# A two-layer linear-attention model on one core: query features of two tiles turned through DRAM and by DVE, and the second layer's output weights asked for at spaced places

## The chip, the core and the metric

The kernel runs on one NeuronCore of a Trainium2 chip. A core has TensorE (PE in the profile; PEld is its weight load, which runs beside the matmuls), VectorE (DVE), ScalarE (ACT), GpSimd (POOL) and SyncE (SP), which only issues transfers here. 16 DMA engines move data between DRAM and the on-chip memory; SP and ACT each have a queue of their own for issuing transfers, and a queue is worked off in order: an issue that waits for a semaphore holds up all issues behind it. The metric is device time in microseconds (us), as the median of several runs.

## What is computed

```python
x = A_x                                        # 1 x 2048 x 576, float32
for layer in range(2):                         # same weights in both layers
    q, k, v = split(layernorm(x) @ wqkv)       # 32 heads of 18
    phi_q = concat(softmax(q @ w_phi), softmax(-q @ w_phi))    # 36 features a head
    phi_k = the same of k
    kv, z = phi_k^T v, sum over rows of phi_k  # over all 2048 rows
    x = x + (phi_q kv) / (phi_q z + 1e-6) @ wo
    x = x + relu(layernorm(x) @ w1 + b1)^2 @ w2 + b2           # 576 -> 4608 -> 576
```

## The kernel before

**Tiles and blocks.** The 2048 rows are four blocks of 512, a block is four tiles of 128 rows. Matmuls run in a 32-bit format with two pieces, high and low, for each operand (names end in h and l), so that a product takes three matmuls.

**Dense parts.** `g_mlp` is the dense part (w1, square, w2) of one block: 36 turns, one for each 128 of the 4608 hidden features, f = 0 to 35. A turn has two steps. In `hidden(f)` PE makes 14 matmuls of 512 columns into one bank `ph` (L955), then ACT takes relu and square (L960, L961) and DVE splits the result (L964, L965). In `second(f-1)` PE multiplies the split result of the turn before by w2 (L980, L972). The weights of a turn come from DRAM on SP's queue: `m_1h` is the chunk of w1 (L918) and `m_1s` that of w2 (L930) in the dense part of block 1, each in two buffers, so a chunk can be loaded when the step that used the chunk two turns before has ended. Only the very first dense part ("fresh", block 3 of layer 0) loads the plain weights (`m_3rr`), splits them on ACT and DVE (L914, L915, L926, L927) and writes the pieces to DRAM for later.

**What is woven in.** While PE works on the dense part of one block, the attention of the next block is woven in. `weave` runs one slot of a `Plan` after each step of the dense part, and a plan's turn is two slots. `plan_attend` puts the calls at turns: query features of the four tiles (`exponents`, `totals`, `scaled`, nearly all DVE), then for each of 5 head groups and 2 signs (i = 0 to 9) the features turned so that features lie on partitions, then `times` (L776) with the blocks of the keys, then `project` (L799) with the output weights wo, then the norm for the block's own dense part. A call with a larger depth stands earlier within its slot. In each engine the order is that of the program, except on SP, whose order a scheduler makes from when it takes each transfer to be ready. There are three such dense parts in each layer (the fourth has no next block). In layer 0 the second and third also hold the keys of the second layer for the block just finished (`plan_keys`).

**The two ways to turn.** In layer 0 `Out.turn` (L714 to L716) transposes the four tiles on PE into a bank, ACT copies the high piece out and DVE makes the low one. In layer 1 a tile makes a trip: `arrange` (POOL) copies the features into a padded tile z, `store` sends z to the DRAM tensor `phs` from ACT's queue (L737), `fetch` brings it back with 32x32 blocks in their place (L742), `flip` lets DVE transpose each 32x32 block (L747), and `pieces` takes high and low pieces of each tile (L756, L757). The fetched tile (`e`) uses the buffers `wraw` and `rr`, in which the output weights come later: `a_0o0h` is the high piece of the first half of wo's columns for block 0, then `a_0o0l`, `a_0o1h`, `a_0o1l` (L315, two transfers each).

Of the kernel before, what the change touches and what calls it, by code (L numbers as in the profile page):

```python
# [7 lines left out]
F32 = mybir.dt.float32  # L8
F32R = mybir.dt.float32r
AF = mybir.ActivationFunctionType  # L10
# [3 lines left out]
P = 128  # L14
TB = 512
NT = TB // P
# [5 lines left out]
def layers_kernel(  # L22
# [18 lines left out]
    nc = tc.nc  # L41
# [653 lines left out]
    class Out:  # L695

        def __init__(self, layer, b, ph, name):
            self.layer, self.b, self.ph, self.name = layer, b, ph, name
            self.f, self.pn, self.x, self.pair = {}, {}, {}, None
            self.z, self.e = {}, {}  # L700

        def turn(self, i, half=None):
            g, s = divmod(i, 2)
# [34 lines left out]
                                    self.z.pop((t, s)).rearrange("p (a f) -> p a f", a=KC))  # L738

        def fetch(self, t):  # L740
            self.e[t] = sb.tile([P, NC * HP], F32, tag=TAGS_C[t % 2], name=f"{self.name}e{t}")
            nc.scalar.dma_start(self.e[t][:, : KC * 2 * NG * 32],  # L742
                                phs[self.b][t].rearrange("a (r k) s f -> (a r) (k s f)", k=KC))

        def flip(self, t):
            e = self.e[t][:, : KC * 2 * NG * 32]
            nc.vector.transpose(e, e)  # L747

        def pieces(self, i):
            g, s = divmod(i, 2)  # L750
            w = gw[g]
            fh, fl = (sb.tile([GW, TB], F32R, tag="ft", name=f"{self.name}f{k}{g}{s}", bufs=4) for k in "hl")
            for t in range(NT):
                src = self.e[t][:w, : KC * 2 * NG * 32].rearrange("p (k n r) -> p k n r", k=KC, r=32)[:, :, s * NG + g]
                hi, lo = (f[:w, t * P : (t + 1) * P].rearrange("p (r k) -> p k r", k=KC) for f in (fh, fl))
                nc.scalar.activation(hi, src, AF.Copy)  # L756
                nc.vector.tensor_sub(lo, src, hi.bitcast(F32))  # L757
            self.f[i] = fh, fl

        def times(self, i, half=None):  # L760
# [56 lines left out]
    def plan_queries(plan, at, gap, layer, raws, er, ph, name):  # L817

        zb = sums[layer]["zb"]
        r = {}  # L820

        def first(t):
            if t == 0:
                r[0] = sb.tile([P, NT, 2, H], F32, tag="rq", name=f"{name}r", bufs=1)
            er.append(exponents(raws[t], f"{name}Q{t}"))

        def second(t):
            e, rt = er[t], r[0][:, t]
            totals(e, rt)
            m = sb.tile([P, 2, D], F32, tag="m", name=f"{name}m{t}", bufs=1)  # L830
            u = sb.tile([P, 2, H], F32, tag="u", name=f"{name}u{t}", bufs=1)
            nc.vector.tensor_mul(m, e, zb)
            nc.vector.tensor_reduce(u, m.rearrange("p s (h d) -> p s h d", d=DH), op=ALU.add, axis=AX.X)
            r[t + 1] = u

        def third(t):
            e, rt, u = er[t], r[0][:, t], r.pop(t + 1)
            nc.vector.tensor_mul(u, u, rt)
            nc.vector.scalar_tensor_tensor(u[:, 0], u[:, 0], DEN_EPS, u[:, 1], op0=ALU.add, op1=ALU.add)
            nc.vector.reciprocal(u[:, 1], u[:, 0])  # L840
            nc.vector.tensor_mul(rt, rt, u[:, 1].unsqueeze(1).to_broadcast([P, 2, H]))
            scaled(e, rt)
            ph.append(e)

        for t in range(NT):
            plan.put(at + gap * t, 0, first, t)
            plan.put(at + gap * t + 1, 1, second, t)
            plan.put(at + gap * t + 2, 2, third, t)
        return at + gap * (NT - 1) + 2

    def plan_attend(plan, at, gap, layer, b, raws, dst, name, o, queries=None):

        out = Out(layer, b, [], name)
        out.pair, calls = o
        if queries:
            for t in range(NT):
                plan.put(at + gap * t, 0, queries, t)
            at += 1
        if layer == 0:
            for n, call in enumerate(calls):  # L860
                plan.put(at + n, 9, call)
        done = at + 2
        at = plan_queries(plan, at, gap, layer, raws, [], out.ph, name) + 1
        if layer:
            for t in range(NT):
                for k, (step, call) in enumerate(((0.5, out.arrange), (1.5, out.store), (2.5, out.fetch), (4, out.flip))):
                    plan.put(done + gap * t + step, -1, call, t)
            at += 3.5
        for i in range(2 * NG):
            plan.put(at + i / 2, 0, out.pieces if layer else out.turn, i)  # L870
            plan.put(at + (i + 1 + layer) / 2, 1, out.times, i)
        if layer:
            for n, call in enumerate(calls):
                plan.put(at + NG + n / 4, 9, call)
            at += 1.5
        at += NG + 1
        for t in range(NT):
            plan.put(at + t - 1, 9, out.load, t)
        trips = range(NT) if layer else range(NT - 1)
# [547 lines left out]
    def body():  # L1427

        order = [NB - 1, NB - 2] + list(range(NB - 2))
        queries, other, o, last_keys = opening()  # L1430
        for layer in range(2):
            q1 = None
            ready, prev_rows, keep = {}, None, {}
            for i, b in enumerate(order):
                n = f"{layer}_{b}"
                nxt, rows = {}, []
                gen = g_mlp(layer, b, ready, rows, f"m{n}", layer == 0 and i == 0, i == 0, layer == 1 and i == NB - 1)
                plan = Plan()
                if i == 0:
                    out = Out(layer, b, [], f"t{layer}o")  # L1440
                    out.pair = o[0]
                    barrier(layer, b, last_keys, queries, other, ready, out, gen)
                    for t in range(NT):
                        plan.on(2 + t, 0, out.keep, t, out.x[t])
                at = 0
                if prev_rows is not None:
                    at = plan_keys(plan, prev_rows, i == NB - 1, keep)
                if i + 1 < NB:
                    nb, n2 = order[i + 1], f"a{layer}_{order[i + 1]}"
                    if i or layer:  # L1450
# [90 lines left out]
```

## Time and profile before

| what | value |
|---|---|
| median of 3 runs | 2523.01 us (2520.92 to 2524.05) |
| profiled execution | 2526.71 us |
| its span, first to last instruction | 2525.0 us |
| mean granted clock of TensorE | 0.996 |
| PE busy | 2495.7 us (99%) |
| DVE, ACT, POOL busy | 1223.7, 769.7, 152.5 us |
| bytes moved | 540.99 MB, mean 214 GB/s |

The profiled execution is 3.7 us above the median and 1.7 us longer than its span. PE is nearly always busy, so the places where it is not, and the instructions that it issues, are what to read; the other engines matter where PE waits for them. The first dense part runs from about 240 to 490 us, the three of layer 1 with a woven attention from about 1465 to 2290 us.

### The profile page before, as it was taken

Reading aid. Unit: us, or ns where it says so; the run is one execution under the profiler, and the core shown is the slowest. Engines: PE = TensorE matmul, PEld = TensorE weight load, DVE = VectorE, ACT = ScalarE, POOL = GpSimd, SP = SyncE. Lnnn points to the kernel's source line nnn. Section 1 sums busy time; section 2 is a strip of 40 time slices with the busy share of each in tenths; the row PEclk is TensorE's granted clock in tenths of the full one; section 3 lists DMA queues with packets and bytes.
Section 4 is the critical chain, followed back from the end, with each engine's and each line's share of the span. In section 5 each row is a group of like instructions: output and inputs, shape, how many; then the busy total and the mean of one; then the engine's idle time right before and its main releaser. Section 6 shows DMA issues by size and latency. Waiting matters only on the chain.

```text
span 2525.0 us, 37453 instructions
## 1 busy us (share of the span) xinstructions
PE 2495.7 (99%) x15084; PEld 2198.6 (87%) x15084; DVE 1223.7 (48%) x2115; ACT 769.7 (30%) x1358; POOL 152.5 (6%) x419
## 2 busy tenths in 40 slices
PE   9999999999999999999999999999999999999999
PEld 8998888898888988888889988788887888888887
DVE  6887955444635446355114776433463426433112
ACT  5544443322222222223223332313223222312221
POOL 4302000000000000000000011000010002000000
PEclk9999999999999999999999999999999999999999
DMA  9514888867648576484564348668575767667665
GB/s 318 175 53 135 288 279 283 307 230 268 215 157 288 179 255 207 165 292 146 193 196 158 130 139 268 215 196 281 177 254 181 259 225 239 206 204 247 197 195 171
DMA packets 196619, 540.99 MB, mean 214 GB/s; under 512 B 26270, under 2 KB 79390, under 8 KB 196446
## 3 DMA queue, kind: packets, MB, share of 16 engines
q1 hardware_dynamic: 163806, 511.06, 60.8%
q10 hardware_dynamic: 32640, 27.53, 3.4%
q8 instruction: 120, 1.97, 0.3%
q14 instruction: 53, 0.43, 0.0%
HBM read 440.12 MB, written 98.40 MB: 213 GB/s over the span
## 4 chain that ended last, share of the span: by engine, by line
PE 97%; DMA 2%; DVE 1%; ACT 0%; issue 0%; SPq 0%; DVEq 0%; ACTq 0%
PE m_2ph L955 9%; PE m_0ph L955 9%; PE m_1ph L955 9%; PE m_3ph L955 9%; PE m_2acc L980 7%; PE m_1acc L980 7%; PE m_3acc L980 7%; PE m_0acc L980 7%; PE m_2acc L972 2%; PE m_1acc L972 2%; PE m_0acc L972 2%; PE m_3acc L972 2%; PE a_0po L799 1%; PE a_2po L799 1%; PE kvp L598 1%; PE a_3po L799 1%
## 5 line engine op out<-in xcount | busy, mean ns | idle before, releaser
L955 PE MATMUL m_0ph<-a_0nh,m_0h 128*128 128x512 f32 x720 | 226.8, 397 | 5.6 <-DMA m_0h<-dw 5.6
L955 PE MATMUL m_2ph<-a_2nh,m_2h 128*128 128x512 f32 x720 | 225.4, 395 | 0.0
L980 PE MATMUL m_1acc<-m_1s,m_1hb 128*128 128x448 f32 x864 | 189.0, 367 | 0.4 <-PE m_1ph L955 0.4
L980 PE MATMUL m_2acc<-m_2s,m_2hb 128*128 128x448 f32 x864 | 189.3, 367 | 0.0
L980 PE MATMUL m_3acc<-m_3s,m_3hb 128*128 128x448 f32 x864 | 188.9, 367 | 0.3 <-DVE m_3hb L964 0.3
L980 PE MATMUL m_0acc<-m_0s,m_0hb 128*128 128x448 f32 x864 | 189.0, 367 | 0.0
L964 DVE CAST m_2hb<-m_2hr 128x512 fp32r<-128x512 f32 x72 | 30.8, 427 | 311.1 <-ACT m_2hr L961 310.7
L980 PEld LDWEIGHTS m_1acc<-m_1s,m_1hb 128*128 128x128 f32 x864 | 161.9, 188 | 18.7 <-PE m_1ph L955 0.5
L980 PEld LDWEIGHTS m_3acc<-m_3s,m_3hb 128*128 128x128 f32 x864 | 161.2, 188 | 17.4 <-PE m_3ph L955 0.5
L980 PEld LDWEIGHTS m_2acc<-m_2s,m_2hb 128*128 128x128 f32 x864 | 160.9, 188 | 16.1
L980 PEld LDWEIGHTS m_0acc<-m_0s,m_0hb 128*128 128x128 f32 x864 | 160.5, 188 | 15.4
L955 PEld LDWEIGHTS m_0ph<-a_0nh,m_0h 128*128 128x128 f32 x720 | 136.1, 189 | 37.4 <-issue 6.2
L964 DVE CAST m_0hb<-m_0hr 128x512 fp32r<-128x512 f32 x72 | 30.8, 428 | 273.4 <-ACT m_0hr L961 273.0
L955 PEld LDWEIGHTS m_2ph<-a_2nh,m_2h 128*128 128x128 f32 x720 | 135.3, 188 | 30.4
L960 ACT ACTIVATE m_0hr<-m_0ph,b1t 128x512 f32<-128x512 f32 x72 | 49.6, 689 | 353.9 <-PE m_0ph L955 343.8
L964 DVE CAST m_1hb<-m_1hr 128x512 fp32r<-128x512 f32 x72 | 30.7, 427 | 260.7 <-ACT m_1hr L961 260.7
L960 ACT ACTIVATE m_2hr<-m_2ph,b1t 128x512 f32<-128x512 f32 x72 | 49.6, 689 | 346.5 <-PE m_2ph L955 346.5
L960 ACT ACTIVATE m_1hr<-m_1ph,b1t 128x512 f32<-128x512 f32 x72 | 49.6, 689 | 324.5 <-PE m_1ph L955 314.4
L960 ACT ACTIVATE m_3hr<-m_3ph,b1t 128x512 f32<-128x512 f32 x72 | 49.6, 689 | 263.4 <-PE m_3ph L955 263.4
L964 DVE CAST m_3hb<-m_3hr 128x512 fp32r<-128x512 f32 x72 | 30.7, 426 | 197.7 <-ACT m_3hr L961 197.7
L955 PE MATMUL m_1ph<-t1onh,m_1h 128*128 128x512 f32 (+1 forms) x380 | 114.2, 387 | 5.6 <-DMA m_1h<-dw 4.9
L955 PE MATMUL m_3ph<-a_3nh,m_3h 128*128 128x512 f32 x360 | 114.7, 401 | 4.4 <-DMA m_3h<-dw 4.4
(1992 smaller groups left out, 5686.6 us busy)
## 6 DMA issues: line engine op xcount, KB each, us to landing
m_2h<-dw SPq DMA_DIRECT2D x72, 640.0 KB
m_0h<-dw SPq DMA_DIRECT2D x72, 640.0 KB
m_1h<-dw SPq DMA_DIRECT2D x72, 640.0 KB
m_2s<-dw SPq DMA_DIRECT2D x72, 576.0 KB
m_0s<-dw SPq DMA_DIRECT2D x72, 576.0 KB
m_1s<-dw SPq DMA_DIRECT2D x72, 576.0 KB
dw<-m_3h SPq DMA_DIRECT2D x36, 640.0 KB
m_3h<-dw SPq DMA_DIRECT2D x36, 640.0 KB
```

What stands on the lines that cost most here:

```text
L598: nc.tensor.matmul(po[32 * q : 32 * q + 32, :, j], vt[:, h * VW : h * VW + 32], e[:, :, h * DH : (h + 1) * DH], start=not stay, stop=True, ...
L799: nc.tensor.matmul(pt[:, :HP], a, m[:w, g], start=(g == 0 and k == 0), stop=(g == NG - 1 and k == 2))
L955: nc.tensor.matmul(ph[:, cols], a, m, start=(k == 0), stop=(k == 3 * KC + 1))
L960: nc.scalar.activation(hr, ph, AF.Relu, bias=b1t[:, f : f + 1])
L964: nc.vector.tensor_copy(hh, hr)
L972: nc.tensor.matmul(acc[KC], a, m, start=(f == 0 and k == 0), stop=(f == NF - 1 and k == 2))
L980: nc.tensor.matmul(acc[t][:, :R], a[:, rows], m, start=(f == 0 and k == 0), stop=(f == NF - 1 and k == 2))
```

## The change

In layer 0 tiles 0 and 1 of each of the three woven attentions now make the trip; tiles 2 and 3 are still transposed on PE, side by side in one bank (`pieces` does both). Their fetched tiles use buffers `v`, one for each sign (640 columns instead of 1280). `times` of layer 0 comes a slot later after its pieces, and all that follows it half a turn later. In layer 1 all four tiles go through DRAM as before; their flip is planned 1 turn after the fetch instead of 1.5, and the four requests for output weights, which stood at +0, +0.25, +0.5 and +0.75 turn, now stand at -0.5, +0.5, +1 and +2; `project` and the norm follow one turn later. In the last two woven dense parts of layer 1 the queries start at turn 5 instead of 6.5, and the four transfers of the normalised rows that they need are put 1 turn apart instead of 1.5.

```diff
         def fetch(self, t):
+            n = NG * 32
+            if len(self.trips) == NT:
+                e = self.e[t, 0] = self.e[t, 1] = sb.tile([P, NC * HP], F32, tag=TAGS_C[t % 2], ...)
...
+            for s in range(2):
+                e = self.e[t, s] = sb.tile([P, KC * n], F32, tag="v", name=f"{self.name}e{t}{s}", bufs=4)
+                nc.scalar.dma_start(e.rearrange("p (k f) -> p k f", k=KC),
+                                    phs[self.b][t][:, :, s].rearrange("a (r k) f -> (a r) k f", k=KC))
...
         def pieces(self, i):
-            for t in range(NT):
+            for t in self.trips:
...
                 nc.scalar.activation(hi, src, AF.Copy)
                 nc.vector.tensor_sub(lo, src, hi.bitcast(F32))
+            if n < NT:
+                pt = wtile(f"{self.name}pt{g}{s}")
+                for t in range(n, NT):
+                    nc.tensor.transpose(pt[:w, t * P : (t + 1) * P], self.ph[t][:, s, g * GW : g * GW + w], ident)
+                nc.scalar.activation(fh[:w, n * P :], pt[:w, n * P :], AF.Copy)
+                nc.vector.tensor_sub(fl[:w, n * P :], pt[:w, n * P :], fh[:w, n * P :].bitcast(F32))
...
+        out.trips = range(NT if layer else 2)
+        back = 2.5 if layer else gap + 0.5
+        for t in out.trips:
+            plan.put(done + gap * t + 0.5, -1, out.arrange, t)
+            plan.put(done + gap * t + 1.5, -1, out.store, t)
+            plan.put(done + gap * t + back, -2, out.fetch, t)
+            plan.put(done + gap * t + back + 1, -1, out.flip, t)
         if layer:
-            at += 3.5
+            at += 3
         for i in range(2 * NG):
-            plan.put(at + i / 2, 0, out.pieces if layer else out.turn, i)
-            plan.put(at + (i + 1 + layer) / 2, 1, out.times, i)
+            plan.put(at + i / 2, 0, out.pieces, i)
+            plan.put(at + i / 2 + 1, 1, out.times, i)
+        at += 0.5
         if layer:
             for n, call in enumerate(calls):
-                plan.put(at + NG + n / 4, 9, call)
-            at += 1.5
+                plan.put(at + NG + (-0.5, 0.5, 1, 2)[n], 9, call)
+            at += 2.5
...
-                        start, step = (at - 4, 0.5) if at else (0, 0.75)
+                        start, step = (at - 4 if at else 0), 0.5
...
-                        plan_attend(plan, at or 6.5, 2, layer, nb, raws2, nxt, n2, o,
+                        plan_attend(plan, at or 5, 2, layer, nb, raws2, nxt, n2, o,
```

**SP, first woven dense part of layer 1.** Issues in SP's queue before (h and s are the weight chunks, the number behind them the turn; o0h to o1l the output weights):

```order
L918 DMA m_1h_23_15739<-dw_23_156 128x1280
L930 DMA m_1s_22_15722<-dw_22_191 128x1152
L315 DMA a_0o0h<-kept_oh 126x1152
L315 DMA a_0o0h<-kept_oh 72x288
L315 DMA a_0o0l<-kept_ol 126x1152
L315 DMA a_0o0l<-kept_ol 72x288
L315 DMA a_0o1h<-kept_oh 126x1152
L930 DMA m_1s_23_15785<-dw_23_192 128x1152
L315 DMA a_0o1h<-kept_oh 72x288
L315 DMA a_0o1l<-kept_ol 126x1152
L315 DMA a_0o1l<-kept_ol 72x288
L918 DMA m_1h_24_15800<-dw_24_157 128x1280
```

And now, in the same place of SP's queue:

```order
L945 DMA m_1h_23_15939<-dw_23_156 128x1280
L315 DMA a_0o0h<-kept_oh 126x1152
L957 DMA m_1s_22_15929<-dw_22_191 128x1152
L315 DMA a_0o0h<-kept_oh 72x288
L315 DMA a_0o0l<-kept_ol 126x1152
L315 DMA a_0o0l<-kept_ol 72x288
L945 DMA m_1h_24_15986<-dw_24_157 128x1280
L957 DMA m_1s_23_15982<-dw_23_192 128x1152
L315 DMA a_0o1h<-kept_oh 126x1152
L315 DMA a_0o1h<-kept_oh 72x288
L945 DMA m_1h_25_16030<-dw_25_158 128x1280
L957 DMA m_1s_24_16028<-dw_24_193 128x1152
```

Chunk h 24 stood behind all four output pieces and s 23; now it stands behind o0h and o0l only and ahead of s 23, o1h stands behind s 23, and o1l comes after s 24. In the two later dense parts of layer 1 the order is the same, with 26 in the place of 24.

**PE, first woven attention of layer 0**, the end of a `second`, the transposes of i = 0 and the start of `hidden(14)`, before:

```order
L972 MATMUL m_3acc_3708<-m_3hb_4330,m_3s_12_4292 128x512 x3
L714 MATMUL a_2pt_4408<-ident,a_2Q0e 126x128
L714 MATMUL a_2pt_4408<-ident,a_2Q1e 126x128
L714 MATMUL a_2pt_4408<-ident,a_2Q2e 126x128
L714 MATMUL a_2pt_4408<-ident,a_2Q3e 126x128
L955 MATMUL m_3ph_4424<-t0onh,m_3h_14_4362 128x512
```

And now:

```order
L999 MATMUL m_3acc_3708<-m_3hb_4374,m_3s_12_4336 128x512 x3
L777 MATMUL a_2pt_4456<-ident,a_2Q2e 126x128
L777 MATMUL a_2pt_4456<-ident,a_2Q3e 126x128
L982 MATMUL m_3ph_4470<-t0onh,m_3h_14_4406 128x512
L982 MATMUL m_3ph_4470<-t0onl,m_3h_14_4406 128x512
```

Two of four transposes are gone in each of 30 groups: PE has 8224 rows instead of 8284.

**DVE, the same attention**, before (L915 makes the low piece of the chunk of w1 for turn 9, L964 and L965 split the square of `hidden(8)`, L927 makes the low piece of the chunk of w2, L561 starts on the features of tile 2):

```order
L915 TENSOR_TENSOR m_3h_9_4087<-m_3rr_4027,m_3h_9_4087 128x640
L964 CAST m_3hb_4109<-m_3hr_4106 128x512
L965 TENSOR_TENSOR m_3hb_4109<-m_3hr_4106,m_3hb_4109 128x512
L927 TENSOR_TENSOR m_3s_9_4127<-m_3rr_4027,m_3s_9_4127 128x576
L561 TENSOR_REDUCE a_2r<-a_2Q2e 128x64
```

And now, with the first flip (the two rows of L757):

```order
L942 TENSOR_TENSOR m_3h_9_4121<-m_3rr_4043,m_3h_9_4121 128x640
L991 CAST m_3hb_4143<-m_3hr_4140 128x512
L992 TENSOR_TENSOR m_3hb_4143<-m_3hr_4140,m_3hb_4143 128x512
L757 STREAM_TRANSPOSE a_2e_4087<-a_2e_4087 128x640
L757 STREAM_TRANSPOSE a_2e_4089<-a_2e_4089 128x640
L954 TENSOR_TENSOR m_3s_9_4165<-m_3rr_4043,m_3s_9_4165 128x576
L561 TENSOR_REDUCE a_2r<-a_2Q2e 128x64
L562 RECIPROCAL a_2r<-a_2r 128x64
```

The fetch that this flip needs is issued on ACT's queue one turn earlier, right behind the square of `hidden(7)`. The flip of tile 1 stands at the same place three turns later.

More of the change, by code (lines that the diff above doesn't have):

```diff
@@ L699, in __init__ @@
             self.f, self.pn, self.x, self.pair = {}, {}, {}, None
-            self.z, self.e = {}, {}
+            self.z, self.e, self.trips = {}, {}, ()
         def turn(self, i, half=None):
@@ L740, in fetch, with turned @@
         def fetch(self, t):
-            self.e[t] = sb.tile([P, NC * HP], F32, tag=TAGS_C[t % 2], name=f"{self.name}e{t}")
-            nc.scalar.dma_start(self.e[t][:, : KC * 2 * NG * 32],
-                                phs[self.b][t].rearrange("a (r k) s f -> (a r) (k s f)", k=KC))
-        def flip(self, t):
-            e = self.e[t][:, : KC * 2 * NG * 32]
-            nc.vector.transpose(e, e)
+            n = NG * 32
+            if len(self.trips) == NT:
+                e = self.e[t, 0] = self.e[t, 1] = sb.tile([P, NC * HP], F32, tag=TAGS_C[t % 2], name=f"{self.name}e{t}")
+                nc.scalar.dma_start(e[:, : KC * 2 * n], phs[self.b][t].rearrange("a (r k) s f -> (a r) (k s f)", k=KC))
+                return
+            for s in range(2):
+                e = self.e[t, s] = sb.tile([P, KC * n], F32, tag="v", name=f"{self.name}e{t}{s}", bufs=4)
+                nc.scalar.dma_start(e.rearrange("p (k f) -> p k f", k=KC),
+                                    phs[self.b][t][:, :, s].rearrange("a (r k) f -> (a r) k f", k=KC))
+        def flip(self, t):
+            if len(self.trips) == NT:
+                e = self.e[t, 0][:, : KC * 2 * NG * 32]
+                nc.vector.transpose(e, e)
+                return
+            for s in range(2):
+                nc.vector.transpose(self.e[t, s], self.e[t, s])
+        def turned(self, t, s, g, w):
+            e = self.e[t, s]
+            if len(self.trips) == NT:
+                return e[:w, : KC * 2 * NG * 32].rearrange("p (k n r) -> p k n r", k=KC, r=32)[:, :, s * NG + g]
+            return e[:w].rearrange("p (k n r) -> p k n r", k=KC, r=32)[:, :, g]
         def pieces(self, i):
             g, s = divmod(i, 2)
-            w = gw[g]
+            w, n = gw[g], len(self.trips)
             fh, fl = (sb.tile([GW, TB], F32R, tag="ft", name=f"{self.name}f{k}{g}{s}", bufs=4) for k in "hl")
-            for t in range(NT):
-                src = self.e[t][:w, : KC * 2 * NG * 32].rearrange("p (k n r) -> p k n r", k=KC, r=32)[:, :, s * NG + g]
+            for t in self.trips:
+                src = self.turned(t, s, g, w)
                 hi, lo = (f[:w, t * P : (t + 1) * P].rearrange("p (r k) -> p k r", k=KC) for f in (fh, fl))
@@ L863, in plan_attend @@
         at = plan_queries(plan, at, gap, layer, raws, [], out.ph, name) + 1
+        out.trips = range(NT if layer else 2)
[5 more added lines that the diff above has]
+            plan.put(done + gap * t + back + 1, -1, out.flip, t)
         if layer:
-            for t in range(NT):
-                for k, (step, call) in enumerate(((0.5, out.arrange), (1.5, out.store), (2.5, out.fetch), (4, out.flip))):
-                    plan.put(done + gap * t + step, -1, call, t)
-            at += 3.5
+            at += 3
         for i in range(2 * NG):
-            plan.put(at + i / 2, 0, out.pieces if layer else out.turn, i)
-            plan.put(at + (i + 1 + layer) / 2, 1, out.times, i)
+            plan.put(at + i / 2, 0, out.pieces, i)
+            plan.put(at + i / 2 + 1, 1, out.times, i)
+        at += 0.5
         if layer:
             for n, call in enumerate(calls):
-                plan.put(at + NG + n / 4, 9, call)
-            at += 1.5
+                plan.put(at + NG + (-0.5, 0.5, 1, 2)[n], 9, call)
+            at += 2.5
         at += NG + 1
```

## The prediction

> **What bounds the kernel.** I read the page's busy times first, then the chain of waits, then who PE waits for.
>
> ```profile
> PE 2495.7 (99%) x15084; PEld 2198.6 (87%) x15084; DVE 1223.7 (48%) x2115; ACT 769.7 (30%) x1358; POOL 152.5 (6%) x419
> PE 97%; DMA 2%; DVE 1%; ACT 0%; issue 0%; SPq 0%; DVEq 0%; ACTq 0%
> ```
>
> PE is busy or on the chain nearly all the time. So two things can shorten the span: instructions that PE no longer issues, and the few waits of PE. What falls on DVE, ACT, POOL or the queues counts only if PE comes to wait for it. PE's longest waits, all of them in layer 1:
>
> ```profile
> PE m_0ph L955 <- DMA m_0h<-dw: 5.6, 1, 5.6
> PE m_1ph L955 <- DMA m_1h<-dw: 4.9, 1, 4.9
> PE m_3ph L955 <- DMA m_3h<-dw: 4.4, 1, 4.4
> PE fp L219 <- DMA fr<-in_A_wqkv: 1.5, 2, 0.8
> ```
>
> Each woven dense part of layer 1 has one wait for a chunk of w1, 4.4 to 5.6 us, and the next largest wait in the kernel is 1.5 us in two pieces. The timeline of PE shows that the wait is not all (first a `hidden` step without a wait and the step behind it, then for each of the three waits the step that waited and the one behind it):
>
> ```profile
> 1629.58 0.40 PE L955 MATMUL m_1ph<-t1onh,m_1h 128*128 128x512 f32 x1
> ...
> 1632.85 2.60 PE L980 MATMUL m_1acc<-m_1s,m_1hb 128*128 128x448 f32 x12
> ...
> 1641.06 0.77 PE L955 MATMUL m_1ph<-t1onh,m_1h 128*128 128x512 f32 x1 [4.92 <-DMA m_1h<-dw]
> ...
> 1646.67 2.60 PE L980 MATMUL m_1acc<-m_1s,m_1hb 128*128 128x448 f32 x12
> ...
> 1942.77 0.76 PE L955 MATMUL m_0ph<-a_0nh,m_0h 128*128 128x512 f32 x1 [5.63 <-DMA m_0h<-dw]
> ...
> 1947.76 0.29 PE L799 MATMUL a_3po<-a_3o0h,a_3oh 126*128 126x288 f32 x1
> ...
> 2217.13 0.76 PE L955 MATMUL m_3ph<-a_3nh,m_3h 128*128 128x512 f32 x1 [4.37 <-DMA m_3h<-dw]
> ...
> 2223.09 0.29 PE L799 MATMUL a_2po<-a_2o0h,a_2oh 126*128 126x288 f32 x1
> ```
>
> A `hidden` of 14 matmuls takes 1632.85 - 1629.58 = 3.27 us. Behind the waits it takes 5.61, 4.99 and 5.96 us. The reason is in the windows (columns: stretch, its length, busy time of PE, PEld, DVE, ACT and POOL, then granted clock, share of the DMA engines, GB/s):
>
> ```profile
> 1638.00:1642.00 4.00, 0.94 (x2) 0.83 (x3) 0.00 (x0) 0.00 (x0) 0.00 (x0) 0.65 0.96 364
> 1642.00:1646.00 4.00, 4.00 (x11) 3.08 (x10) 0.00 (x0) 0.00 (x0) 0.00 (x0) 0.50 0.14 54
> ```
>
> After the wait the granted clock is 0.50 for the whole of 1642 to 1646, so PE pays a second time. The Trainium skill, "TensorE: Matmul & The Clock Gate", Part 1, says that the clock falls to half once PE has been idle for a window of about 3.4 us; the three waits, all longer, agree with it.
>
> Why the chunk is late stands in SP's queue (issues; the chunk that waits is the last row):
>
> ```profile
> 1623.66 0.76 SPq L315 DMA_DIRECT2D a_0o0h<-kept_oh  x2
> ...
> 1629.07 0.34 SPq L930 DMA_DIRECT2D m_1s<-dw  x1
> ...
> 1630.74 0.35 SPq L918 DMA_DIRECT2D m_1h<-dw  x1
> ```
>
> The output weights go out as soon as the fetched tiles are free; then the queue stands still until 1629.07, when PE ends the `second` that frees a buffer for m_1s; m_1h, whose own buffer was free when the `hidden` before had ended (about 1625), is issued only at 1630.74 and lands when PE starts, at 1641. So it is late twice: 5.4 us in the queue, then 10 us behind a full set of transfers.
>
> **The change, part by part.**
>
> *Output weights spaced.* h 24 (26 in the two later parts) now stands behind o0h and o0l only, ahead of the s that blocked it. How long it takes is worked out from sizes:
>
> ```profile
> m_1h<-dw SPq DMA_DIRECT2D x3, 640.0 KB
> m_1s<-dw SPq DMA_DIRECT2D x4, 576.0 KB
> a_0o0h<-kept_oh SPq DMA_DIRECT2D x1, 567.0 KB
> a_0o0h<-kept_oh SPq DMA_DIRECT2D x1, 81.0 KB
> ```
>
> From the issue of o0h on there lie two pieces of 648 KB, one s of 576 KB and h itself with 640: 2512 KB or 2.57 MB, at the 364 GB/s of the window above 7.1 us. Between o0h's issue and the `hidden` that needs this h lie more than two steps of dense part with their `times`: before, 1623.66 to 1636 (wait begins), 12.3 us, and now the same or more, since the pieces end just after a `hidden` and h is needed by the third `hidden` after it. So it arrives about 5 us early. The next two chunks each have one s and one output piece (1224 KB, 3.4 us) ahead of them and a turn to come in: 3.27 us of `hidden` and as much of `second` (1632.85 to 1641.06 - 4.92 = 1636.14), 6.6 us. o1l goes out two turns before `project` needs it, about 13 us. I take all three waits as gone: 4.92 + 5.63 + 4.37 = 14.92 us, and the slow matmuls with them: (5.61 - 3.27) + (4.99 - 3.27) + (5.96 - 3.27) = 6.75 us. Together 21.7 us; the bounds are 0 (another chunk is late by as much) and 21.7.
>
> *Transposes on PE.* Three attentions of layer 0 times 10 groups lose two of four transposes: 60. Their price is the spacing of starts, not the duration:
>
> ```profile
> 326.11 0.27 PE L714 MATMUL a_2pt<-ident,a_2Q0e 128*126 128x128 f32 x1
> ...
> 326.44 0.27 PE L714 MATMUL a_2pt<-ident,a_2Q3e 128*126 128x128 f32 x1
> ```
>
> 0.33 us for three steps, 0.11 us each, so 60 x 0.11 = 6.6 us off PE. That time is on the path, because PE is.
>
> *Pieces in layer 0 on ACT and DVE.* Before and now, for one group:
>
> ```profile
> L715 ACT ACTIVATE a_0fh<-a_0pt x10: 579/594/599, 685.2 to 723.2; 126x512 fp32r<-126x512 f32 x8, 72x512 fp32r<-72x512 f32 x2
> L756 ACT ACTIVATE a_0fh<-a_0e x40: 416/440/449, 1589.0 to 1623.2; 126x128 fp32r<-126x128 f32 x32, 72x128 fp32r<-72x128 f32 x8
> L715 ACT ACTIVATE t0of<-t0opt x20: 370/382/391, 200.7 to 221.3; 126x256 fp32r<-126x256 f32 x16, 72x256 fp32r<-72x256 f32 x4
> 335.00:345.00 10.00, 10.00 (x53) 8.67 (x52) 5.08 (x9) 5.33 (x9) 0.00 (x0) 1.00 0.92 299
> ```
>
> ACT: 0.59 us becomes 2 x 0.44 + 0.38 = 1.26, so +6.7 us an attention; DVE's subtractions follow ACT's pieces and grow alike. This falls in some 40 us in which ACT is busy 5.33 of 10 us and DVE 5.08 (the last row). `times` now has two slots instead of one behind its pieces. I cost it at nothing; if the cover went, PE would wait in `times`, at most 6.7 us an attention.
>
> *Stores, fetches, flips in layer 0.* POOL's arranging (POOL stands idle in these rows) costs nothing. The place to watch is the first dense part, where DVE is nearly full:
>
> ```profile
> 285.00:295.00 10.00, 10.00 (x47) 8.57 (x47) 8.47 (x13) 5.01 (x7) 0.00 (x0) 1.00 0.84 270
> 295.00:305.00 10.00, 10.00 (x47) 8.46 (x46) 9.29 (x16) 3.95 (x6) 0.00 (x0) 1.00 0.76 278
> L747 DVE STREAM_TRANSPOSE a_0e<-a_0e x4: 1503/1504/1511, 1529.0 to 1586.1; 128x1280 f32<-128x1280 f32 x4
> 290.71 0.76 DVE L927 TENSOR_TENSOR m_3s<-m_3rr,m_3s 128x576 fp32r<-128x576 f32 x1 [1.13 <-ACT m_3s L926]
> 291.77 1.35 DVE L561 TENSOR_REDUCE a_2r<-a_2Q2e 128x64 f32<-128x1152 f32 x1 [0.30 <-ACT a_2Q2e L558]
> ...
> 297.41 0.69 DVE L965 TENSOR_TENSOR m_3hb<-m_3hr,m_3hb 128x512 fp32r<-128x512 f32 x1
> 281.20 0.63 ACT L961 ACTIVATE m_3hr<-m_3hr 128x512 f32<-128x512 f32 x1
> 299.62 0.69 ACT L960 ACTIVATE m_3hr<-m_3ph,b1t 128x512 f32<-128x512 f32 x1 [1.89 <-PE m_3ph L955]
> ```
>
> A flip of 1280 columns takes 1.50 us; two of 640 I put at 1.6. The first one stands just in front of L927 at 290.71, where DVE idles 1.13 us and, a step on, 0.30. Behind it waits the split that ends at 297.41 + 0.69 = 298.1, which PE needs when `hidden(10)` is over, at 299.6 (ACT's relu of it starts then). So DVE may run 1.5 us late there before PE waits. If the fetched tile is there, DVE runs 1.6 - 1.43 = 0.2 us late and PE loses nothing. Whether it is there: the fetch goes out behind ACT's square, at 281.8, and DVE reaches the flip at 290.71 - 1.13 = 289.6, 7.8 us later. The one fetch of which the trace shows the landing:
>
> ```profile
> 1577.80 0.34 ACTq L742 DMA_DIRECT2D a_0e<-phs  x1
> 1586.07 1.51 DVE L747 STREAM_TRANSPOSE a_0e<-a_0e 128x1280 f32<-128x1280 f32 x1 [2.17 <-DMA a_0e<-phs]
> ```
>
> took 8.27 us for the same 640 KB. At that length the flip starts 0.5 us late, DVE is 0.7 us late, PE still does not wait. The lower end is 0; for the upper end I let the fetch take half as long again, 12.4 us: DVE is 4.8 us late and PE 3.3 us, at two flips 6.6 us. I take 0.7 us, near the lower end, since the measured row falls there. In the other two dense parts of layer 0 I cost the flips at nothing: there are no fresh weights to split there, so DVE idles in each turn.
>
> *The rest of layer 1* (queries at turn 5, flip half a turn sooner, project a turn later) moves calls between slots. It takes no instruction from PE and adds none; what the queries need was loaded without a wait before, and a flip half a turn sooner still stands between the same two squares. Cost 0.
>
> **Sum.** 21.7 + 6.6 - 0.7 = 27.6 us off the profiled execution, 2526.7 to 2499.1. The median of the runs lies 3.7 us lower, so 2523.0 - 27.6 = 2495.4; I say 2495.5 us, 1.1% faster. A difference under 0.2%, 5 us, I count as none, which is about what a measurement of this kernel can tell.
>
> **Rivals.**
>
> *A wait stays or moves.* For it: the four pieces are still 2.6 MB within three turns, beside weights, and the DMA engines ran at 0.96 in the window above. Against it: the 5 us of spare time. One wait that stays at its old size costs 4.4 to 5.6 plus 1.7 to 2.7, about 7.3 us: 2503; two: 2510. By the skill's rule above, a remainder of less than about 3.4 us could escape the half clock and cost only itself, which would put a single one at 2499 or below; no row here shows such a short wait.
>
> *The pieces or flips take the place of the transposes.* PE then waits in the first dense part for a late split, or in `times`. With the upper end of 6.6 us for the flips the time is 2501; if each of 30 `times` waited as long as it saves, 6.6 us again, 2502. For it: DVE at 9.29 of 10. Against it: the margins of 1.5 us, and the attentions of layer 1, which make four trips and show no wait of PE for pieces.
>
> *Slower.* The place is the first dense part, from the first store to the second flip. A turn there is (299.62 + 0.69 - 281.20) / 3 = 6.4 us (from the square of `hidden(7)` to the end of the relu of `hidden(10)`). The store goes two turns ahead of the fetch at 281.8, the second flip comes three turns behind the first: 269 to 311 us, 42 us. The DMA engines are 0.84 busy at 270 GB/s, and two stores and two fetches add 4 x 655 kB = 2.6 MB, 62 GB/s, so the share becomes 0.84 x 332 / 270 = 1.03. If the raw weights fall behind, PE waits for a chunk in turn after turn, each time 7.3 us with the half clock. It decides from four such turns on (29 us against 28.3 saved), of the six or seven in the stretch: 2524 us or more. The row that is nearest:
>
> ```profile
> ACT m_3s L926 <- DMA m_3rr<-in_B_w: 5.3, 3, 1.8
> ```
>
> ACT waits for raw weights three times, at most 1.8 us, and PE never for ACT there, so the loads have room. The Trainium skill, "DMA: Bandwidth & Descriptors", "Issuing engines are not separate DMA queues", says that transfers issued by ACT run on the same 16 engines as SP's: by that rule the trips do take time from the weights, and this rival is possible; that 2.6 MB against a spare share of 0.16, 51 GB/s or 2.2 MB in 42 us, overfills by only 0.4 MB speaks against it.
>
> That the change does nothing is out: the order has the 60 transposes gone and the chunk ahead of the blocking issue.
>
> **Chances.** Forecast (2493 to 2499) 0.70; a wait that stays or moves in layer 1, one or two of three (2501 to 2511), 0.14; pieces or flips in the first layer (2499 to 2503), 0.10; all gain given back in the first dense part, within 5 us of before or slower, 0.06. The low end is 28.3 us less with none of the 0.7 lost, and the 2 us by which the fastest run undercuts the median: 2492.5. The high end takes in one wait that stays and some of the flips, 2506. Faster by over 0.2%: 0.94; within: 0.03; slower: 0.03.
>
> **What would show it.** In the new profile: no wait of PE over 3 us for an m_h chunk in layer 1 and no window at clock 0.50 there; 60 transposes fewer under L777 and L714 together; h 24 issued within 1 us of the end of its `hidden`. The flips of the first dense part would show their wait for phs: under 1.5 us each if I am right. I am wrong if PE waits for m_3hb or m_3h near 290 to 320 us, or if a chunk in layer 1 is still behind output weights.

## The result, and the profile after

| | before | changed |
|---|---|---|
| median of the runs | 2523.26 us (5 runs, 2520.92 to 2526.85) | 2502.10 us (5 runs, 2499.91 to 2511.49) |
| profiled execution, its span | 2526.71, 2525.0 us | 2501.07, 2499.0 us |
| PE busy in it | 2495.7 us | 2482.7 us |

The ratio of the times is 0.992 (95% interval 0.9899 to 0.9941), so the kernel is 0.8% faster. The forecast was 2495.5 us, 6.6 us too low; its range of 2492 to 2506 holds the result, but the narrower band of 2493 to 2499, to which it gave a chance of 0.70, does not. In two later comparisons on other occasions the changed kernel had medians of 2501.64 and 2501.88 us, so the gap to the forecast is real.

First the page (busy times, then the chain of waits) and PE's longest waits in the new profile:

```profile
PE 2482.7 (99%) x15024; PEld 2187.3 (88%) x15024; DVE 1245.7 (50%) x2187; ACT 779.4 (31%) x1418; POOL 175.2 (7%) x491
PE 96%; DMA 2%; DVE 1%; ACT 1%; issue 0%; ACTq 0%; SPq 0%; DVEq 0%
```

```profile
PE m_0ph L982 <- ACT m_0hr L987: 1.8, 1, 1.8
...
PE m_2ph L982 <- ACT m_2hr L987: 0.7, 1, 0.7
...
PE m_1ph L982 <- DMA m_1h<-dw: 0.3, 1, 0.3
```

The three chunk waits of 4.4 to 5.6 us are gone; of 14.9 us a wait of 0.3 us is left. PE has 60 instructions fewer. Two waits are new, 1.8 and 0.7 us, and they are not for a transfer but for ACT's relu.

SP's queue and PE, first woven dense part of layer 1 (timeline; h is L945, s is L957, L315 the output weights):

```profile
1617.64 0.33 SPq L315 DMA_DIRECT2D a_0o0h<-kept_oh  x1
...
1620.13 0.77 SPq L315 DMA_DIRECT2D a_0o0l<-kept_ol  x2
1621.91 0.34 SPq L945 DMA_DIRECT2D m_1h<-dw  x1
1625.75 0.34 SPq L957 DMA_DIRECT2D m_1s<-dw  x1
1626.19 0.78 SPq L315 DMA_DIRECT2D a_0o1h<-kept_oh  x2
1629.02 0.34 SPq L945 DMA_DIRECT2D m_1h<-dw  x1
```

```profile
1621.03 0.85 PE L982 MATMUL m_1ph<-t1onh,m_1h 128*128 128x512 f32 x3
...
1638.76 0.47 PE L982 MATMUL m_1ph<-t1onh,m_1h 128*128 128x512 f32 x1 [0.30 <-DMA m_1h<-dw]
```

Chunk h 24 is issued at 1621.91, when the `hidden` that used its buffer has just ended (1621.03 + 0.85 = 1621.88), and the `hidden` that needs it starts at 1631.94 without a wait. The chunk behind it, h 25, is issued at 1629.02 and PE needs it at 1638.46: it takes 9.7 us and is 0.30 us late. So the chunk waits are gone, but for h 25 there is no margin. The windows (columns as in the prediction):

```profile
1620.00:1640.00 20.00, 19.70 (x90) 16.38 (x89) 3.95 (x7) 4.45 (x7) 0.00 (x0) 1.00 1.00 274
...
1638.00:1642.00 4.00, 3.70 (x17) 2.71 (x16) 0.00 (x0) 0.00 (x0) 0.00 (x0) 1.00 1.01 245
1642.00:1646.00 4.00, 4.00 (x23) 3.60 (x22) 1.12 (x2) 1.32 (x2) 0.00 (x0) 1.00 0.89 325
```

The clock is 1.00 where it was 0.50, and the DMA engines are full for 20 us at 274 GB/s.

In the first dense part of layer 0, DVE around the first flip (L757) and the window:

```profile
288.43 0.69 DVE L992 TENSOR_TENSOR m_3hb<-m_3hr,m_3hb 128x512 fp32r<-128x512 f32 x1
289.04 1.56 DVE L757 STREAM_TRANSPOSE a_2e<-a_2e 128x640 f32<-128x640 f32 x2
290.52 0.72 DVE L954 TENSOR_TENSOR m_3s<-m_3rr,m_3s 128x576 fp32r<-128x576 f32 x1
```

```profile
285.00:305.00 20.00, 20.00 (x92) 17.06 (x91) 19.35 (x30) 8.97 (x13) 0.36 (x2) 1.00 1.03 351
```

The flips start without a wait, DVE is 97% busy (19.35 of 20 us), the DMA share is 1.03 (0.80 before in the same stretch), and PE is busy for all 20 us.

### The profile page after: what moved, and what is told of

Its sections match the earlier page's. It is cut to its first block, busy times and chain, and to the rows that moved or that the text cites. A ratio compares the mean times of both kernels' runs of the same rounds, so it can differ in the third digit from the quotient of the medians.

```text
span 2499.0 us, 37604 instructions
## 1 busy us (share of the span) xinstructions
PE 2482.7 (99%) x15024; PEld 2187.3 (88%) x15024; DVE 1245.7 (50%) x2187; ACT 779.4 (31%) x1418; POOL 175.2 (7%) x491
## 4 chain that ended last, share of the span: by engine, by line
PE 96%; DMA 2%; DVE 1%; ACT 1%; issue 0%; ACTq 0%; SPq 0%; DVEq 0%
PE m_3ph L982 9%; PE m_1ph L982 9%; PE m_0ph L982 9%; PE m_2ph L982 9%; PE m_3acc L1007 7%; PE m_1acc L1007 7%; PE m_2acc L1007 7%; PE m_0acc L1007 7%; PE m_3acc L999 2%; PE m_1acc L999 2%; PE m_2acc L999 2%; PE m_0acc L999 2%; PE a_0po L821 1%; PE a_2po L821 1%; PE kvp L598 1%; PE a_1po L821 1%
## 5 line engine op out<-in xcount | busy, mean ns | idle before, releaser
L982 PE MATMUL m_3ph<-t0onh,m_3h 128*128 128x512 f32 (+1 forms) x380 | 112.9, 384 | 0.6 <-ACT t0onh L390 0.5
```

The source lines that it names most:

```text
L982: nc.tensor.matmul(ph[:, cols], a, m, start=(k == 0), stop=(k == 3 * KC + 1))
```

## The experiments

**Which part of the change carries the gain.** Theory A: the terms of the prediction are right in the profile, and the median is off because the kernel before varies. Theory B: the gain of the first layer is eaten there. Four kernels with one part each, on one chip; their kernel before had a median of 2525.41 us (29 runs, 2517.06 to 2527.55).

Layer 0 alone (the changed kernel with these lines of layer 1 put back):

```diff
...
-    at += 3
+    at += 3.5
-    plan.put(at + NG + (-0.5, 0.5, 1, 2)[n], 9, call)
-    at += 2.5
+    plan.put(at + NG + n / 4, 9, call)
+    at += 1.5
...
-    plan_attend(plan, at or 5, 2, ...)
+    plan_attend(plan, at or 6.5, 2, ...)
```

> Only the first layer's part of the change (two of four tiles turned through DRAM and by DVE); the second layer as before. Theory A, the terms are sized right and the new small waits of PE for the relu cost what the profile shows (1.8 and 0.7 us): 6.6 less for 60 transposes, 2.5 back, so about 4 us less than before, 2519; the three chunk waits of layer 1 stay, 15 us together. Theory B, the turns' gain is eaten by waits in layer 0 and the whole gain of the change lies in layer 1: no difference, 2523.

Measured: 2524.12 us (12 runs, 2516.88 to 2531.47), ratio 0.9995 (0.9984 to 1.0006): no gain that can be seen. Its page and PE's waits:

```profile
PE 2489.3 (99%) x15024; PEld 2190.8 (87%) x15024; DVE 1243.8 (49%) x2187; ACT 778.4 (31%) x1418; POOL 174.4 (7%) x491
```

```profile
PE m_1ph L982 <- DMA m_1h<-dw: 7.1, 2, 6.6
PE m_3ph L982 <- DMA m_3h<-dw: 5.0, 1, 5.0
PE m_0ph L982 <- DMA m_0h<-dw: 4.8, 2, 4.6
PE a_1pt L777 <- DVE a_1Q3e L571: 1.5, 1, 1.5
...
PE m_2ph L982 <- ACT m_2hr L987: 1.4, 1, 1.4
PE a_0pt L777 <- DVE a_0Q3e L571: 1.2, 1, 1.2
```

PE is 6.4 us less busy (2495.7 - 2489.3), near the 6.6 us of 60 transposes; but both kernels also have slow matmuls behind their chunk waits in this time, so it is no clean price. Against it stand 1.5 + 1.4 + 1.2 = 4.1 us of new waits, and the chunk waits of layer 1, which this kernel does not touch, are 16.9 us in all here and were 14.9. The rest is not told apart from their variation.

Layer 1 alone (the kernel before with the lines on the left side of that diff, and flip half a turn sooner):

> Only the second layer's part (spaced requests for output weights, queries at turn 5, flip half a turn sooner); 60 transposes stay in the first layer. Theory A: the three waits are gone, 2498.7 + 6.6 - 2.5 over the median of the changed kernel, about 2506, 17 us less than before. Theory B: the whole 21 us, 2502. In the profile under both: no wait of PE for an m_h chunk over 1 us in layer 1 and PE busy about 2489 us.

Measured: 2505.19 us (6 runs, 2504.04 to 2506.72), ratio 0.992 (0.9907 to 0.9932), 20.2 us less. Its page:

```profile
PE 2490.3 (99%) x15084; PEld 2196.3 (88%) x15084; DVE 1225.5 (49%) x2115; ACT 770.6 (31%) x1358; POOL 153.8 (6%) x419
```

PE is 5.4 us less busy than before with the same 15084 instructions, and no wait for a chunk is longer than 0.3 us. So layer 1 carries nearly all of the gain, and the spread of the runs falls with it, from 10.5 to 2.7 us.

Only the spacing, and only the earlier queries:

```diff
-    plan.put(at + NG + n / 4, 9, call)
-    at += 1.5
+    plan.put(at + NG + (-0.5, 0.5, 1, 2)[n], 9, call)
+    at += 2.5
```

> Only the four places of the output weights' requests (-0.5, +0.5, +1, +2) and project a turn later; queries stay at turn 6.5, flip as before. If the spacing alone carries the gain: all three waits gone, 2506. If the queries' half turn matters too, since from 6.5 the requests fall behind the other step of a turn and the order has chunk h 28 still behind o1h in the two later dense parts: only the first wait goes (4.9 + 2.3 us), 2515, and the waits for m_0h and m_3h stay over 3 us.

```diff
-    start, step = (at - 4, 0.5) if at else (0, 0.75)
+    start, step = (at - 4 if at else 0), 0.5
...
-    plan_attend(plan, at or 6.5, 2, ...)
+    plan_attend(plan, at or 5, 2, ...)
```

> Only the queries of the last two woven dense parts of layer 1 at turn 5 instead of 6.5, their rows 1 turn apart; the requests for output weights as before (+0, +0.25, +0.5, +0.75). If the requests' bunching alone makes the waits: nothing changes, 2523, with three waits of 4 to 6 us, now at turn 26 instead of 28. If the queries' place matters by itself: two waits smaller, 2509 at best.

Measured: spacing alone 2523.51 us (12 runs, ratio 0.9995, 0.9985 to 1.0006); queries alone 2529.94 us (12 runs, ratio 1.0019, 1.0010 to 1.0028), a little slower. Neither theory had these times: the first is 8.5 us off its nearer one, the second 7 us. PE's waits, spacing alone:

```profile
PE m_0ph L955 <- DMA m_0h<-dw: 3.6, 1, 3.6
PE m_3ph L955 <- DVE a_3nl L457: 3.5, 1, 3.5
PE m_2ph L955 <- DVE a_2nl L457: 2.8, 1, 2.8
```

and queries alone:

```profile
PE m_3ph L955 <- DMA m_3h<-dw: 7.4, 1, 7.4
PE m_1ph L955 <- DMA m_1h<-dw: 6.1, 1, 6.1
PE m_0ph L955 <- DMA m_0h<-dw: 5.1, 1, 5.1
```

Spacing alone does remove two of the three chunk waits; one of 3.6 us stays. But with project a turn later and the queries still at 6.5, the norm of the next block ends after its dense part (a_3nl, a_2nl at L457), and PE waits there instead. The earlier queries alone leave the bunched requests and all three chunk waits; why these are larger there than before (18.6 us) was not found, and m_1h lies in a part that this edit does not change. The two edits of layer 1 only work together: the spacing costs a turn at the end, and the earlier queries give it.

**Is the bunching needed for the waits?** The changed kernel with only the four places back at +0, +0.25, +0.5, +0.75. On this occasion the kernel before had 2523.6 us (15 runs).

```diff
-    plan.put(at + NG + (-0.5, 0.5, 1, 2)[n], 9, call)
+    plan.put(at + NG + n / 4, 9, call)
```

> The changed kernel with the four requests for output weights at +0, +0.25, +0.5, +0.75 turn again; project and everything else stays. If the spacing carries the gain of layer 1: three waits of 5 us for m_h chunks are back with the half clock, 2502 + 20 = 2522. If the earlier queries, the later project or the flip carry it: 2502.

Measured: 2523.83 us (11 runs, 2517.61 to 2532.47), ratio 0.9998 (0.9986 to 1.0009). The whole gain is gone, by PE's three waits, 15.7 us, and the slow matmuls behind them (PE busy 2489.3 us, where the changed kernel has 2483.4 on this occasion): 21.6 us together, against 22.2 between the two medians.

```profile
PE m_1ph L982 <- DMA m_1h<-dw: 7.1, 1, 7.1
PE m_0ph L982 <- DMA m_0h<-dw: 5.1, 1, 5.1
PE m_3ph L982 <- DMA m_3h<-dw: 3.5, 1, 3.5
```

The changed kernel itself, on the same occasion and the next:

> The changed kernel once more, beside the others on one chip. Theory A (the terms in the profile are right; the kernel before varies with the size of its chunk waits): 2500 to 2503 in most executions, about 23 us under a kernel before at 2525. If the margin of the third chunk is as thin as the 0.3 us wait shows, an execution in five or so is near 2510, with one chunk wait long enough to halve the clock; if the 2511 was a disturbance from outside, none is.

> The changed kernel, beside the three others on one chip: 2500 to 2503.

Measured: 2501.64 us (4 runs, 2500.16 to 2502.07) and 2501.88 us (5 runs, 2500.28 to 2504.95). Of its 14 runs in all one was near 2510 (2511.49, with a mean clock of 0.998 against 1.0 of the others), not one in five. That a chunk wait with the half clock came back in it fits the missing margin; the run was not profiled, so it is not shown. The two profiles taken here show how the margin varies: in the first no chunk of w1 is late, in the second one by 1.8 us (m_3h), at a clock that stays at 1.00.

**Where the new waits for relu come from.** First theory: ACT stands at a fetch of phs whose store has not landed.

```diff
-    back = 2.5 if layer else gap + 0.5
+    back = 2.5 if layer else 3.5
```

> The changed kernel with fetch and flip of the second and third dense parts of layer 0 one turn later. If PE's waits for relu there (0.7 and 1.8 us) come from ACT standing at a fetch whose store has not landed: they are gone, 2.5 us less, 2499.6. If they come from the full DMA engines in another way (a late weight, DVE): they stay, 2502, or the flip, now one turn before the pieces, makes PE wait in times for as much.

Measured: 2502.20 us (4 runs), and the waits stay (m_0ph 1.9 us in two, m_2ph 0.7). The theory had the wrong place, and the edit made ACT's queue worse: the fetch of tile 0 now stands right behind the store of tile 1 and holds ACT (timeline of ACT, third dense part):

```profile
962.49 1.44 ACTq L737 DMA_DIRECT2D phs<-a_1z  x2
964.30 7.55 ACTq L748 DMA_DIRECT2D a_1e<-phs  x2
971.90 0.69 ACT L987 ACTIVATE m_0hr<-m_0ph,b1t 128x512 f32<-128x512 f32 x1 [9.06 <-DMA phs<-a_1z]
```

The waits are not there but at the end of the dense part, in the norm. ACT and PE of the changed kernel:

```profile
1077.94 0.45 ACTq L424 DMA_DIRECT2D xrm<-a_1nr  x1
...
1092.33 0.34 ACTq L435 DMA_DIRECT2D a_1nn<-xrm  x1
1092.71 1.10 ACT L456 ACTIVATE a_1nh<-a_1nn 128x512 fp32r<-128x512 f32 x1 [8.19 <-DMA xrm<-a_1nr]
...
1093.93 0.66 ACT L987 ACTIVATE m_0hr<-m_0ph,b1t 128x512 f32<-128x512 f32 x1
```

```profile
1094.65 0.50 PE L982 MATMUL m_0ph<-a_0nh,m_0h 128*128 128x512 f32 x1 [1.80 <-ACT m_0hr L987]
```

The norm makes the same kind of trip through DRAM. Its last store goes out at 1077.94, the fetch stands in ACT's queue until 1092.33, 14.4 us later, and the relu behind it is late for PE. In the three profiles of the changed kernel and that of the failed theory ACT is idle 6.1 to 8.2 us at these fetches, and PE's wait follows it with a fixed difference of 6.4 us: 8.19 us give 1.80, 7.56 give 1.19, 7.07 give 0.69, 6.89 give 0.52, and 6.08 give none. The change had put project and norm of layer 0 half a turn later; so that half turn was taken back:

```diff
-    at += 0.5
+    at += 0.5 * layer
```

> The changed kernel without the half turn by which project and the norm of layer 0 came later (in layer 1 as changed). The waits of PE for the relu stand at the end of the second and third dense parts of layer 0, where ACT is held 8.2 us by the norm's last fetch. If the half turn makes them: m_0ph and m_2ph waits of 1.8 and 0.7 us gone, 2499 to 2500 against 2501.6 of the changed kernel. If the trips' two extra stores and fetches or the weights of the keys make them: they stay, 2501 to 2502.

Measured: 2500.92 us (5 runs, 2499.02 to 2509.65), on an occasion where the changed kernel had 2501.88 and the kernel before 2523.83. Both waits for relu are gone, and ACT no longer stands at the fetch with a relu behind it; ACT now:

```profile
1081.98 0.34 ACTq L435 DMA_DIRECT2D a_1nn<-xrm  x1
1084.80 0.69 ACT L987 ACTIVATE m_0hr<-m_0ph,b1t 128x512 f32<-128x512 f32 x1 [4.01 <-PE m_0ph L982]
```

The mechanism is shown; in time it gives 1.0 us, not told apart from none: two of the five runs are at 2504.60 and 2509.65, with mean clocks of 0.999 and 0.998, and the profiled execution has other waits of PE of the same size:

```profile
PE a_1pt L777 <- DVE a_1Q3e L571: 1.9, 1, 1.9
...
PE m_1ph L982 <- DMA m_1h<-dw: 0.9, 1, 0.9
```

**A version that beats both.** The wait of the transposes for tile 3's features (a_1Q3e) comes and goes: 0, 1.4 and 0 us in the three profiles of the changed kernel in the order of this text, 1.9 us in the kernel just above. What stands ahead of it in ACT's queue is the fetch of tile 1 (ACT of the changed kernel, third dense part):

```profile
972.28 3.03 ACTq L748 DMA_DIRECT2D a_1e<-phs  x2
975.40 0.69 ACT L987 ACTIVATE m_0hr<-m_0ph,b1t 128x512 f32<-128x512 f32 x1 [5.38 <-PE m_0ph L982]
```

The relu starts 0.1 us after the two issues are through (972.28 + 3.03 = 975.31), and exponents and DVE follow it. So, besides the norm, this fetch alone and its flip were put a turn later, that of tile 0 left where it was:

```diff
+    late = 0 if layer or gap == 3 else t
-    plan.put(done + gap * t + back, -2, out.fetch, t)
-    plan.put(done + gap * t + back + 1, -1, out.flip, t)
+    plan.put(done + gap * t + back + late, -2, out.fetch, t)
+    plan.put(done + gap * t + back + late + 1, -1, out.flip, t)
```

> As the one without the half turn, and in the second and third dense parts of layer 0 the fetch and flip of tile 1 (not of tile 0) one turn later, so that ACT does not stand 2 to 3 us at it. Expected: besides the waits for relu, that of the transposes for tile 3 (a_1Q3e, 0 to 1.5 us in the four profiles) gone: 2498.5 to 2499.5. If flips one turn before the pieces are too late: PE waits there, 2500 to 2503.

Measured: 2497.93 us (4 runs, 2497.31 to 2499.39), ratio to before 0.9895 (0.9882 to 0.9909). All four lie under all five of the changed kernel on that occasion. The fetch (third dense part) no longer holds up a relu, and the waits of PE for a relu in layer 0 and for tile 3 are gone; a new one of 1.6 us is for a chunk of w1 (m_2h, at 502 us). The last row is PE's: the `hidden` of the relu at 982.22 ends at 981.32 + 0.86 = 982.18, so the relu starts 0.04 us behind it, although its row names the fetch:

```profile
977.17 1.22 ACTq L748 DMA_DIRECT2D a_1e<-phs  x2
982.22 0.69 ACT L988 ACTIVATE m_0hr<-m_0ph,b1t 128x512 f32<-128x512 f32 x1 [3.94 <-DMA a_1e<-phs]
981.32 0.86 PE L983 MATMUL m_0ph<-a_0nh,m_0h 128*128 128x512 f32 x3
```

That the wait for tile 3 comes from this fetch is borne out by five profiles: the relu behind it starts 0.42, 0.73 and 0.44 us after the end of its `hidden` in the changed kernel, 1.38 us with the norm's repair and 0.03 us here, and PE's waits are 0, 1.4, 0, 1.9 and 0 us. That the whole 3.0 us between the last two medians are these waits is not shown: the wait is at most 1.9 us, and the two profiled executions are 1.5 us apart.

An earlier try with one output piece a turn (places -0.5, +1, +2, +3, project a turn later still, queries at turn 4, and the fetches of the failed theory) was slower than the changed kernel:

> A version that may beat both: fetch and flip of layer 0 a turn later as above, output weights at -0.5, +1, +2, +3 with project a turn later, and the queries of the last two parts at turn 4, so that the norm is not later than now. One output piece for each turn: chunk waits and executions near 2510 gone. Expected 2499, without the spread of the changed kernel. If the norm's place at the end of the dense part, or the rows for the queries at turn 4, is the next limit, PE waits there 2 to 4 us and it is 2503 to 2508.

Measured: 2505.41 us (5 runs, 2503.40 to 2506.75). No chunk of w1 is late there, but PE's waits show that it pays at the end of a dense part,

```profile
PE m_1py L1088 <- ACT m_1yt L1066: 1.6, 1, 1.6
```

and for relu and transposes in layer 0 (1.6 + 1.3 + 1.0 + 1.0 us), where it has the fetches of the failed theory.

**The price of the first layer's part**, beside the changed kernel on one chip:

> Only the second layer's part again, beside the others on one chip, to price the first layer's part. By the sum of profile terms (6.6 us of transposes less 2.5 of new waits): 4 us above the changed kernel, 2505.5. If the transposes gain nothing: 2502. If they gain all of it: 2508.

Measured: 2505.17 us (5 runs, 2503.53 to 2505.79) against 2501.88: 3.3 us. So of 6.6 us of transposes about half arrives, near the 4 us of theory A. The profiles agree: from layer 1 alone (two) to the changed kernel (three) PE's busy time falls by 7.5 us, from 2490.3 to 2482.8 in the mean, and its idle time in the span rises by 2.6 us, from 13.5 to 16.1. With the two repairs above it is 7.2 us (2505.17 - 2497.93), all of it.

## Why the prediction was right and wrong

*Output weights spaced (21.7 us).* Right in mechanism and in size. Layer 1 alone has it by itself: its profiled span is 20.8 us shorter (2525.0 to 2504.2). 5.4 us of that is busy time of PE, for which 6.75 us of slow matmuls were forecast, and 15.4 us is idle time, for which 14.9 were forecast. The medians gave 20.2 us.

*The margin of the chunks.* The 5 us were said of h 24; PE does not wait for it, and when it lands the trace does not show. The thin place is the next chunk. For h 25 the prediction put 3.4 us for the 1224 KB ahead of it against 6.6 us; its own 640 KB at the same 364 GB/s make it 5.2 us. It had 9.4 us and took 9.7, so this step was wrong: the rate came from a window of 4 us, and the full engines moved 274 GB/s over 20 us. At that rate the 1864 KB make 7.0 us; the rest of the 9.7 is not accounted for. The margin was nothing, -0.3 us. The waits went because the time to come in was also longer than forecast, which is luck.

*Transposes (6.6 us).* Right for PE, and a little small: 7.5 us less busy. That this and the slow matmuls miss by about 1 us each in opposite directions, so that the sum comes out, is luck. Only 3.3 us of it reached the medians, for the reason two points below. The pieces that take their place cost PE no wait that is seen in `times`; ACT's busy time rose by 9.7 us in all (769.7 to 779.4), not by 6.7 us in each of three attentions.

*Pieces and flips in the first dense part (0 and 0.7 us).* The flips cost nothing, and no wait of theirs shows. The rival by which this part becomes slower did not come: over its 42 us (269 to 311) the DMA share is 1.01 at 344 GB/s, near the 1.03 and 332 GB/s worked out for it, and PE is busy for all 42 us. The Trainium skill's rule in "DMA: Bandwidth & Descriptors", "Issuing engines are not separate DMA queues", is borne out by that share, which was 0.81 before; full engines alone did not delay PE.

*"Flips in the other two dense parts of layer 0 at nothing".* This step failed. The price was sought at DVE, and it lay in ACT's queue: a fetch that waits for its store holds the relu behind it, in the trips (at 972 us) and, by the half turn that all that follows got, in the norm (1.8 + 0.7 us in the first profile; 0.5 + 0.6 in the second, which has 1.4 us at the trips). "It moves calls between slots. Cost 0" was said of layer 1 alone; for layer 0 the half turn was not priced at all.

*"The rest of layer 1: cost 0".* As a sum it held, as a reading it did not: without the earlier queries the spacing gives nothing, since the norm then comes 3.5 and 2.8 us too late and one chunk wait of 3.6 us stays.

*The step to the median.* This made the larger part of the 6.6 us. The profiled execution less the terms was 2526.7 - 27.6 = 2499.1; with the new waits (2.5) and without the 0.7 it is 2500.9, and that execution came out at 2501.07. The prediction then took off another 3.7 us because the median lay lower. But the runs of the kernel before seem to differ by the size of the very waits that the change takes away: they spread over 10.5 us with the waits and over 2.7 and 2.3 without them (layer 1 alone, twice), and the fastest of the 29, at 2517.06 us, has a mean clock of 0.999, those above 2527 us 0.996 or 0.997. These runs were not profiled, so it is an inference. What a change leaves has to be reached from the execution in which the waits were read, not from a run that had less of them.

*Rivals.* "A wait stays" would have been 2503 or more; at most one of 14 runs looks like it, and one of five with the norm's repair (2509.65). "Pieces or flips take the place of the transposes" gave the right time, 2501 to 2502, by another place: ACT's queue, not DVE or `times`. That its time came out is chance.

## What to carry to other kernels

Take a wait's whole price off the execution in which it was read, and do not also take off the distance to the median: where runs vary, the waits can be what varies, as they seem to be here. When an edit moves a whole tail of calls by half a turn, look at each in-order queue for a fetch that now comes sooner behind its store or behind more traffic; the engine that issues it stands, whatever else it has to do. Two edits that look like separate gains can be one: check each alone, here both were worth nothing or less by themselves.

## What was unexpected of the hardware

A wait need not be as long as the three of the kernel before to halve the clock. With spacing alone, PE stands still for 2.83 us at the end of the last woven dense part (PE, then windows):

```profile
2287.64 0.79 PE L955 MATMUL m_2ph<-a_2nl,m_2h 128*128 128x512 f32 x1 [2.83 <-DVE a_2nl L457]
```

```profile
2287.00:2288.00 1.00, 0.36 (x1) 0.36 (x2) 0.97 (x2) 0.00 (x0) 0.00 (x0) 0.80 0.91 327
2288.00:2289.00 1.00, 1.00 (x3) 0.80 (x3) 0.24 (x1) 0.00 (x0) 0.00 (x0) 0.50 1.02 394
...
2291.00:2292.00 1.00, 1.00 (x5) 0.83 (x5) 0.00 (x0) 0.00 (x0) 0.00 (x0) 0.99 0.79 244
```

The clock is 0.50 for some 3 us after it, while after the 1.80 us at 1094 it stayed at 1.00. "TensorE: Matmul & The Clock Gate", Part 1, of the Trainium skill has a window of about 3.4 us; the prediction's rival, that a remainder under 3.4 us costs only itself, does not hold here. In the 14 traces of this case each of the 15 waits of PE of 2.83 us or more during the dense parts has the half clock in it or behind it, and none of the 10 of 1.22 to 1.88 us has. The length of the wait does not set the moment: the clock falls 2.0 us after the wait begins in one case (spacing alone, 2009.13 us) and 5.2 us after in another (queries alone, 1636.62 us).

The other thing is the rate of full DMA engines: at a share of 1.00 to 1.04 windows of this kernel show from 245 (1638 to 1642 us, above) to 414 GB/s (1085 to 1090 us), so one window's rate is no measure for another stretch.
